# A decode kernel's last weight: W_O loaded in 16, 6, 7, 2, 1 rows, with one piece shared unevenly among the DMA engines

## The chip, the core and the metric

The kernel runs on one core of a Trainium2 chip. The metric is device microseconds (us) of one execution. Before the change three runs gave a median of 195.58 us (195.41 to 195.92).

## The reference

One decoding step of a transformer block in which attention and feed-forward stand side by side: both read the same layer-normed input, and both results are added to `x`. There are 4 sequences, model width 512, 32 query heads over 8 key/value heads of width 128, a window of the last 4096 positions, and a SwiGLU feed-forward of width 1792. All tensors are bf16.

```python
xn = layernorm(x)                                  # 4 x 512
q  = xn @ wq                                       # 4 x 32 heads x 128
k, v = k_cache[:, :, -4096:], v_cache[:, :, -4096:]   # 8 kv heads, each for 4 query heads
o  = softmax(q @ k.T * 128**-0.5) @ v              # per head
a  = o.reshape(4, 4096) @ wo                       # wo: 4096 x 512
f  = (silu(xn @ w_gate) * (xn @ w_up)) @ w_down
return x + a + f
```

The core reads 81 MB from memory, nearly all of it keys and values; `wo` is 4 MB of it.

## The kernel before, in words

The kernel is written engine by engine, with semaphores placed by hand; no scheduler reorders anything. Inside one block each engine has its own program. SP issues every large load in a fixed order: W_Q, then the key and value loads of 16 pairs (kv head, two sequences), each 2 MB, with W_G and W_U among the first and W_down among the last, and at the end W_O. A load is split over the core's 16 DMA engines, and each of them works through its share of all loads in the order of issue. Loads are issued so far ahead that the DMA engines always have work.

TensorE runs, for every pair, transposes of the keys, the scores, the row maximum and P·V, and then the tail: the last pair, the gate and up matmuls, the W_down matmuls, the transposes that put the attention output into the tile `OP`, and the W_O product. The latter is `out_rows`: W_O lies in SBUF as `WO`, 128 partitions by 32 rows `c` of 512 columns (1 KB a row), and for each row `c` two matmuls of 256 columns add `OP[:, c, :]` times that row into the accumulator `ps_acc`. The five pieces in which W_O is loaded are cut at `WO_CUTS`, each with a semaphore of its own `d_wo[n]`, and `out_rows` waits for a piece where its first row comes.

TensorE does the first piece, 16 rows, inside the block. Then come two matmuls whose result nobody reads (`spin`), the end of the block, at which all engines wait for each other, and behind it the other rows. After the last of them VectorE and ScalarE each copy half of `ps_acc` to `y`, and ScalarE's queue stores `y`.

Names used later: `load_wo` issues the pieces of W_O on SP's queue; `d_wo0` to `d_wo4` are their semaphores; `s_op` says that `OP` is written. In the profile the W_O matmuls are `ps_acc<-wo_sb,oP` on line 193, spin matmuls are `ps_s<-kbuf,ident`, and the end of the block is line 197. The load of the W_O pieces stands on line 251.

Of the kernel before, what the change touches and what calls it, by code (L numbers as in the profile page):

```python
# [12 lines left out]
def bass_parallel_sum__sliding_block_cached__swiglu_ffn__decode_kernel(  # L13
# [10 lines left out]
    out: bass.AP,  # L24
):
    B, _, D = A_x.shape
    _, HKV, Sk, Dh = A_k_cache.shape
    HQ = A_wq.shape[1] // Dh
    F = B_w_gate.shape[1]
# [18 lines left out]
    NO = HQ * Dh // 128  # L48
# [11 lines left out]
    WO = sb("wo_sb", [128, NO, D], BF16)  # L60
# [54 lines left out]
    def sem(name):  # L115
        return nc.alloc_semaphore(name=name)
# [3 lines left out]
    d_wu = sem("d_wu")  # L120
    d_wd = sem("d_wd")
    d_out = sem("d_out")
    WO_CUTS = (0, 16, 26, 29, 31, 32)
    d_wo = [sem("d_wo%d" % q) for q in range(len(WO_CUTS) - 1)]
    d_k = [sem("d_k%d" % s) for s in range(2)]
    d_v = [sem("d_v%d" % s) for s in range(2)]
# [30 lines left out]
    s_acc = sem("s_acc")  # L157
# [8 lines left out]
    wo_ap = A_wo.rearrange("(p c) n -> p c n", c=NO)  # L166
# [6 lines left out]
    def load(eng, to, rows, pieces):  # L173


        with nc.discard():
            by_row = eng.dma_start(to, rows).ins
        whole = replace(by_row.ins[0], ap=pieces.ap, bass_ap=pieces)
        return eng.add_instruction(replace(by_row, name=nc.get_next_instruction_name(), ins=[whole],
                                           ant_dge_precooked=False))  # L180

    def fold_rows(w):
        return w.rearrange("(p c) n -> p (c n)", p=32)

    def load_kv(eng, buf, cache, d):
        return load(eng, buf[:, d % 2 * KVN:(d % 2 + 1) * KVN], kv_ap(cache, d, 1), kv_ap(cache, d, FOLD))

    def out_rows(eng, c0, c1):
        for c in range(c0, c1):
            if c in WO_CUTS:  # L190
                eng.wait_ge(d_wo[WO_CUTS.index(c)], 16)
            for n in range(2):
                last = eng.matmul(ps_acc[64 * n:64 * n + B, 0:256], OP[:, c, :], WO[:, c, 256 * n:256 * n + 256],  # L193
                                  start=False, stop=True, skip_group_check=True)
        return last

    with nc.Block() as block:
# [40 lines left out]
        @block.sync  # L238
        def _(eng):
            def load_k(d):  # L240
                if d >= 2:
                    eng.wait_ge(s_tr, 2 * NG * (d - 1))
                load_kv(eng, KB, A_k_cache, d).then_inc(d_k[d % 2], 16)

            def load_v(d):
                eng.wait_ge(s_pv, d + 1)
                load_kv(eng, VB, A_v_cache, d).then_inc(d_v[d % 2], 16)

            def load_wo(n):
                a, b = WO_CUTS[n], WO_CUTS[n + 1]  # L250
                eng.dma_start(WO[:, a:b, :], wo_ap[:, a:b, :]).then_inc(d_wo[n], 16)

            eng.dma_start(WQ[:], wq_ap).then_inc(d_wq, 16)

            eng.wait_ge(s_xc, 1)
            load_k(0)
            load_k(1)
            load(eng, WG[:], wg_ap, fold_rows(B_w_gate)).then_inc(d_wg, 16)
            load(eng, WU[:], wu_ap, fold_rows(B_w_up)).then_inc(d_wu, 16)
            load_v(0)  # L260
            for d in range(2, ND):
                load_k(d)
                load_v(d - 1)
            load(eng, WD[:], wd_ap, fold_rows(B_w_down)).then_inc(d_wd, 16)
            load_v(ND - 1)
            for n in range(len(d_wo)):
                load_wo(n)
# [99 lines left out]
        def _(eng):  # L367
            def mm(o, l, r, start=False, stop=True):
                return eng.matmul(o, l, r, start=start, stop=stop, skip_group_check=True)  # L369
# [65 lines left out]
            def spin(n):  # L435

                for _ in range(n):
                    mm(ps_S[0][:], ident[:], KB[:, 0:512], start=True)
# [6 lines left out]
            with eng.Fori(0, ND // 2) as r:  # L445
                for b in range(2):
                    n = 2 * r + (b + 1)
# [45 lines left out]
            last.then_inc(s_pm, 1)  # L493
            spin(1)
            eng.wait_ge(s_op, 1)
            out_rows(eng, 0, WO_CUTS[1])
            spin(2)

            eng.br_lt(flag, 1, on_true="tensor_tail", on_false="tensor_never")
            with nc.body("tensor_never", valid_engines=[mybir.EngineType.PE]):  # L500
# [2 lines left out]

    out_rows(nc.tensor, WO_CUTS[1], NO).then_inc(s_acc, 1)
    nc.vector.wait_ge(s_acc, 1)
    nc.vector.tensor_copy(y[:, 0:256], ps_acc[0:B, 0:256]).then_inc(s_y, 1)  # L508
    nc.scalar.wait_ge(s_acc, 1)
# [32 lines left out]
```

## Time and profile before

| what | value |
|---|---|
| median of three runs | 195.58 us (195.41 to 195.92) |
| the profiled execution's own time | 195.48 us |
| its span, first to last instruction | 194.2 us |
| TensorE busy | 163.6 us (84%) |
| VectorE busy | 115.2 us (59%) |
| DMA over the span | 81.09 MB, mean 417 GB/s |
| granted TensorE clock, mean | 0.991 |

The span leaves out 1.3 us of the execution's own time, at its two ends. TensorE's busy share is not TensorE at its peak. DMA rates are those of all 16 DMA engines together; a rate over a stretch counts a packet where it starts or lands, so for stretches under a microsecond it is rough. A row of the timeline gives start and length in us, the engine (PE is TensorE's matmul side, PEld its weight load, SPq the queue of DMA issues on SP), line, operation and tiles, a count, and in brackets the idle time before it and who ended it.

### The profile page before, as it was taken

Reading aid. Unit: us, or ns where it says so; the run is one execution under the profiler, and the core shown is the slowest. Engines: PE = TensorE matmul, PEld = TensorE weight load, DVE = VectorE, ACT = ScalarE, POOL = GpSimd, SP = SyncE. Lnnn points to the kernel's source line nnn. Section 1 sums busy time; section 2 is a strip of 40 time slices with the busy share of each in tenths; the row PEclk is TensorE's granted clock in tenths of the full one; section 3 lists DMA queues with packets and bytes.
Section 4 is the critical chain, followed back from the end, with each engine's and each line's share of the span. In section 5 each row is a group of like instructions: output and inputs, shape, how many; then the busy total and the mean of one; then the engine's idle time right before and its main releaser. Section 6 shows DMA issues by size and latency. Waiting matters only on the chain. (4 is left out here: it accounts for less than half of the span.)

```text
span 194.2 us, 7753 instructions
## 1 busy us (share of the span) xinstructions
PE 163.6 (84%) x3462; PEld 141.4 (73%) x3463; DVE 115.2 (59%) x250; ACT 17.0 (9%) x27; POOL 10.5 (5%) x23
## 2 busy tenths in 40 slices
PE   0137999749999989898989898989898989898895
PEld 0112979648989888787878887888788878787663
DVE  1004858517677767676767676767676767675530
ACT  6600010100110101010101010101010101010100
POOL 8930000000000000000000000000000000000000
PEclk9999999988999999999999999999999999999999
DMA  6999997999999999999999999999999999999992
GB/s 217 432 432 432 511 452 326 432 430 439 425 432 432 439 432 432 432 432 439 439 432 432 432 432 432 432 432 439 432 439 432 439 432 432 432 442 429 395 407 94
DMA packets 3589, 81.09 MB, mean 417 GB/s; under 512 B 664, under 2 KB 800, under 8 KB 1056
## 3 DMA queue, kind: packets, MB, share of 16 engines
q1 hardware_dynamic: 3568, 81.01, 97.3%
q8 instruction: 4, 0.07, 0.1%
q10 hardware_dynamic: 16, 0.01, 0.0%
q14 instruction: 1, 0.01, 0.0%
HBM read 81.01 MB, written 0.00 MB: 417 GB/s over the span
## 5 line engine op out<-in xcount | busy, mean ns | idle before, releaser
L311 DVE COPY kT<-ps_kt 128x1024 bf16<-128x1024 bf16 x128 | 79.8, 683 | 28.0 <-PE ps_kt L397 28.0
L397 PE MATMUL ps_kt<-ident,kbuf 128*128 128x128 bf16 x1024 | 65.5, 224 | 11.2 <-DMA kbuf<-in_A_k_cache_dram 10.3
L397 PEld LDWEIGHTS ps_kt<-ident,kbuf 128*128 128x128 bf16 x1024 | 59.9, 101 | 16.5 <-issue 16.5
L369 PE MATMUL ps_o<-p,vbuf 128*128 128x64 bf16 x1120 | 38.4, 193 | 0.0
L369 PEld LDWEIGHTS ps_s<-qz,kT 128*128 128x128 bf16 x1024 | 31.4, 98 | 7.2 <-issue 4.2
L369 PE MATMUL ps_s<-qz,kT 128*128 x1024 | 34.8, 192 | 1.6 <-issue 0.4
L369 PEld LDWEIGHTS ps_o<-p,vbuf 128*128 128x128 bf16 x1120 | 35.2, 98 | 1.1
L282 ACT ACTIVATE p<-ps_s 128x512 bf16<-128x512 f32 x17 | 10.1, 597 | 162.0 <-PE ps_s L369 162.0
L316 DVE TENSOR_REDUCE rm<-ps_s 128x8 bf16<-128x512 f32 x17 | 11.8, 692 | 20.2 <-PE ps_s L369 20.2
L369 PE MATMUL ps_o<-p,ones 128*128 128x128 bf16 (+1 forms) x69 | 7.0, 222 | 2.1 <-DVE qz L302 1.3
L369 PE MATMUL ps_kt<-wq_sb,xnT 128*32 128x512 bf16 x32 | 3.6, 629 | 5.4 <-DMA wq_sb<-in_A_wq_dram 5.4
L369 PEld LDWEIGHTS ps_o<-p,ones 128*128 128x128 bf16 x69 | 4.5, 98 | 3.4 <-issue 2.2
L369 PE MATMUL ps_s<-mkc,mkr 2*128 2x512 bf16 x17 | 6.8, 398 | 0.0
L374 PE MATMUL ps_acc<-i,xn 4*128 4x4 f32 x4 | 0.6, 254 | 7.1 <-ACT xn L279 7.1
L369 PE MATMUL ps_s<-dg,ones 8*128 8x512 bf16 x17 | 6.5, 385 | 0.0
L369 PEld LDWEIGHTS ps_kt<-wq_sb,xnT 128*32 128x32 bf16 x32 | 1.2, 138 | 7.0 <-issue 7.0
L299 DVE STREAM_TRANSPOSE kT<-ps_kt 128x512 f32<-128x512 f32 x2 | 1.4, 717 | 8.1 <-PE ps_kt L369 8.1
L327 DVE TENSOR_REDUCE den<-ps_o 128x8 f32<-128x128 f32 x18 | 5.0, 276 | 1.7 <-PE ps_o L369 1.7
L374 PEld LDWEIGHTS ps_acc<-i,xn 4*128 4x128 f32 x4 | 0.6, 207 | 7.0 <-issue 7.0
L233 POOL MEMSET vbuf<- 128x6144 f32 x1 | 5.2, 5222 | 0.0
L321 DVE TENSOR_REDUCE m<-ps_acc 8x1 f32<-8x128 f32 x17 | 4.6, 270 | 0.3 <-PE ps_acc L369 0.3
L331 DVE TENSOR_TENSOR oT<-ps_o,den 128x8 f32 (+1 forms) x18 | 3.0, 167 | 2.9 <-issue 2.7
(68 smaller groups left out, 49.2 us busy)
## 6 DMA issues: line engine op xcount, KB each, us to landing
kbuf<-in_A_k_cache_dram SPq DMA_DIRECT2D x16, 2048.0 KB, 12.5
vbuf<-in_A_v_cache_dram SPq DMA_DIRECT2D x16, 2048.0 KB, 11.2
wq_sb<-in_A_wq_dram SPq DMA_DIRECT2D x1, 4096.0 KB, 12.1
wo_sb<-in_A_wo_dram SPq DMA_DIRECT2D x1, 2048.0 KB, 14.9
wg_sb<-in_B_w_gate_dram SPq DMA_DIRECT2D x1, 1792.0 KB, 24.3
wu_sb<-in_B_w_up_dram SPq DMA_DIRECT2D x1, 1792.0 KB, 27.7
wd_sb<-in_B_w_down_dram SPq DMA_DIRECT2D x1, 1792.0 KB, 14.9
wo_sb<-in_A_wo_dram SPq DMA_DIRECT2D x1, 1280.0 KB, 17.3
```

What stands on the lines that cost most here:

```text
L233: eng.memset(VB[:, HKN:].bitcast(FP32), 0.0)
L282: eng.activation(P[:, d % 2 * PS:d % 2 * PS + SN], ps_S[d % 2][:], ACT.Exp, scale=SCALE).then_inc(s_p, 1)
L299: eng.transpose(qT[:, 512 * n:512 * n + 512], ps_kt[n][:])
L311: eng.tensor_copy(KT[:, u * HKN + 1024 * g:u * HKN + 1024 * (g + 1)], kt_ps[g].rearrange("p a b -> p (a b)")).then_inc(s_ev, 1)
L316: eng.tensor_reduce(RM[:], ps_S[bank][:].rearrange("p (t c) -> p c t", c=C), AX.X, ALU.max).then_inc(s_rm, 1)
L321: eng.tensor_reduce(m8[:], mt_ps, AX.X, ALU.max)
L327: eng.tensor_reduce(den[:], den_ps.rearrange("p (t c) -> p c t", c=C), AX.X, ALU.add)
L331: eng.tensor_tensor(OT[:, 2 * b:2 * b + 2, ds(r * REP, REP)], O_ps.rearrange("p (j h) -> p j h", j=2), den[:].rearrange("p (j h) -> p j h" ...
L369: return eng.matmul(o, l, r, start=start, stop=stop, skip_group_check=True)
L374: last = eng.transpose(xT_ps[:, c * B:(c + 1) * B], xn[:].rearrange("b (p c) -> b c p", c=NC)[:, c, :], I4[:])
L397: last = eng.transpose(kt_ps[g][:, k, :], KB[:, a:a + 128], ident[:])
```

## The change

W_O is cut at rows 16, 22, 29, 31 in place of 16, 26, 29, 31: the second piece has 6 rows and the third 7, where there were 10 and 3. The 6-row piece is loaded by five DMAs in place of one: every second partition from 0 (64 of them), every fourth from 1 (32), every eighth from 3 (16), and then the 16 partitions 7, 15, ... 127, which are left, in two DMAs whose access patterns are written so that the first 15 are split over five DMA engines, three partitions each, and partition 127 over three engines, a third each. All five add to one semaphore, and the wait is for 80. On TensorE the first 22 rows stand inside the block, where it was 16, and the two spin matmuls behind them are gone.

```diff
-    WO_CUTS = (0, 16, 26, 29, 31, 32)
+    WO_CUTS = (0, 16, 22, 29, 31, 32)
+    WO_SHARES = (1, 5, 1, 1, 1)
...
+    def shared_load(eng, to, rows, k):
+        with nc.discard():
+            by_row = eng.dma_start(to, rows).ins
+        n = to.shape[0]
+        m = to.shape[1] * to.shape[2]
+        s, t = by_row.ins[0].ap[0][0], by_row.outs[0].ap[0][0]
+        if n > 1:
+            of, at = [[n // k * s, k], [s, n // k], [1, m]], [[t, n], [1, 1], [1, m]]
+        else:
+            of, at = [[m // k, k], [1, 1], [1, m // k]], [[t, 1], [m // k, k], [1, m // k]]
+        return eng.add_instruction(replace(by_row, name=nc.get_next_instruction_name(),
+                                           ins=[replace(by_row.ins[0], ap=of, bass_ap=None)],
+                                           outs=[replace(by_row.outs[0], ap=at, bass_ap=None)],
+                                           ant_dge_precooked=False))
...
     def out_rows(eng, c0, c1):
...
-                eng.wait_ge(d_wo[WO_CUTS.index(c)], 16)
+                n = WO_CUTS.index(c)
+                eng.wait_ge(d_wo[n], 16 * WO_SHARES[n])
...
             def load_wo(n):
                 a, b = WO_CUTS[n], WO_CUTS[n + 1]
-                eng.dma_start(WO[:, a:b, :], wo_ap[:, a:b, :]).then_inc(d_wo[n], 16)
+                if WO_SHARES[n] == 1:
+                    eng.dma_start(WO[:, a:b, :], wo_ap[:, a:b, :]).then_inc(d_wo[n], 16)
+                    return
+                for p, step in ((0, 2), (1, 4), (3, 8)):
+                    eng.dma_start(WO[p::step, a:b, :], wo_ap[p::step, a:b, :]).then_inc(d_wo[n], 16)
+                shared_load(eng, WO[7:120:8, a:b, :], wo_ap[7:120:8, a:b, :], 5).then_inc(d_wo[n], 16)
+                shared_load(eng, WO[127:128, a:b, :], wo_ap[127:128, a:b, :], 3).then_inc(d_wo[n], 16)
...
             eng.wait_ge(s_op, 1)
-            out_rows(eng, 0, WO_CUTS[1])
-            spin(2)
+            out_rows(eng, 0, WO_CUTS[2])
...
-    out_rows(nc.tensor, WO_CUTS[1], NO).then_inc(s_acc, 1)
+    out_rows(nc.tensor, WO_CUTS[2], NO).then_inc(s_acc, 1)
```

SP's program at its end, before the change. The shape is partitions by elements, and `wo_sb` is W_O's tile:

```order
34 L177 DMA wd_sb<-in_B_w_down_dram 128x7168
35 L177 DMA vbuf<-in_A_v_cache_dram 128x1x8192
36 L251 DMA wo_sb<-in_A_wo_dram 128x8192
37 L251 DMA wo_sb<-in_A_wo_dram 128x5120
38 L251 DMA wo_sb<-in_A_wo_dram 128x1536
39 L251 DMA wo_sb<-in_A_wo_dram 128x1024
40 L251 DMA wo_sb<-in_A_wo_dram 128x512
```

And with the change, from the same place:

```order
36 L272 DMA wo_sb<-in_A_wo_dram 128x8192
37 L275 DMA wo_sb<-in_A_wo_dram 64x3072
38 L275 DMA wo_sb<-in_A_wo_dram 32x3072
39 L275 DMA wo_sb<-in_A_wo_dram 16x3072
40 L188 DMA wo_sb<-in_A_wo_dram 15x1x3072
41 L188 DMA wo_sb<-in_A_wo_dram 1x3x1024
42 L272 DMA wo_sb<-in_A_wo_dram 128x3584
43 L272 DMA wo_sb<-in_A_wo_dram 128x1024
44 L272 DMA wo_sb<-in_A_wo_dram 128x512
```

The 16-row piece is issued first in both; behind it five DMAs stand for the second piece, and the pieces of 7, 2 and 1 rows follow as nine issues in all.

TensorE's program around the end of the block (the branch on line 197), before the change, where `oP` is `OP`:

```order
85 L369 MATMUL ps_s<-kbuf,ident 128x512
86 L193 MATMUL ps_acc<-wo_sb,oP 4x256 x32
87 L369 MATMUL ps_s<-kbuf,ident 128x512 x2
88 L499 COMPARE_AND_BRANCH
89 L501 COMPARE_AND_BRANCH
90 L197 UNCONDITIONAL_BRANCH
91 L193 MATMUL ps_acc<-wo_sb,oP 4x256 x32
```

And with it:

```order
85 L395 MATMUL ps_s<-kbuf,ident 128x512
86 L213 MATMUL ps_acc<-wo_sb,oP 4x256 x44
87 L524 COMPARE_AND_BRANCH
88 L526 COMPARE_AND_BRANCH
89 L217 UNCONDITIONAL_BRANCH
90 L213 MATMUL ps_acc<-wo_sb,oP 4x256 x20
```

Twelve W_O matmuls have moved from behind the end of the block to ahead of it, in the place of the two spin matmuls.

## The prediction

> **What bounds the kernel now.** The change touches the last 8 us alone, so I read the timeline of both TensorE queues there first. Each row is start, length, engine, line, tiles, count, and in brackets what ended the idle time before it.
>
> ```profile
> 187.81 1.62 PEld L193 LDWEIGHTS ps_acc<-wo_sb,oP 128*4 128x4 bf16 x32 [0.51 <-DVE oP L364]
> 187.81 1.91 PE L193 MATMUL ps_acc<-wo_sb,oP 128*4 128x256 bf16 x32 [0.21 <-DVE oP L364]
> 189.65 0.60 PE L369 MATMUL ps_s<-kbuf,ident 128*128 128x512 bf16 x2
> 190.53 1.66 PEld L193 LDWEIGHTS ps_acc<-wo_sb,oP 128*4 128x4 bf16 x32 [0.76 <-DMA wo_sb<-in_A_wo_dram]
> 190.56 1.91 PE L193 MATMUL ps_acc<-wo_sb,oP 128*4 128x256 bf16 x32 [0.30 <-PEq L197]
> 192.10 0.08 PEld L193 LDWEIGHTS ps_acc<-wo_sb,oP 128*4 128x4 bf16 x2
> 192.51 0.41 DVE L508 CAST y_sb<-ps_acc 4x256 bf16<-4x256 f32 x1 [4.75 <-PE ps_acc L193]
> ```
>
> The first 32 W_O matmuls (16 rows) start at 187.81, when `OP` is there. The spin pair runs until 190.25, then all engines meet, and the other 32 begin with the weight load at 190.53. The last two weight loads come at 192.10, the row that waits for the one-row piece; the copies start at 192.51. Everything after 192.10 is a fixed train: two matmuls, the copies, the store. So the time is set by when 192.10 can be.
>
> Two things could set it. The first is TensorE. One matmul lasts 272 ns in the grouped rows, so 32 of them in 1.91 us start (1.91 - 0.272) / 31 = 0.053 us apart.
>
> ```profile
> L193 PE MATMUL ps_acc<-wo_sb,oP 128*4 128x256 bf16 x64 | 3.8, 272 | 0.5 <-PEq L197 0.3 <-DVE oP L364 0.2
> ```
>
> From 190.53 on, 30 matmuls ahead of the last two take 30 x 0.053 = 1.59, which gives 192.12. The second is the load. The SP queue's rows give the issue, the issue rows the time from there to landing:
>
> ```profile
> 172.17 2.49 SPq L251 DMA_DIRECT2D wo_sb<-in_A_wo_dram  x5
> 172.80 0.43 SPq L251 DMA_DIRECT2D wo_sb<-in_A_wo_dram  x1
> 173.27 0.91 SPq L251 DMA_DIRECT2D wo_sb<-in_A_wo_dram  x2
> 174.22 0.43 SPq L251 DMA_DIRECT2D wo_sb<-in_A_wo_dram  x1
> wo_sb<-in_A_wo_dram SPq DMA_DIRECT2D x1, 2048.0 KB, 14.9
> wo_sb<-in_A_wo_dram SPq DMA_DIRECT2D x1, 1280.0 KB, 17.3
> wo_sb<-in_A_wo_dram SPq DMA_DIRECT2D x1, 384.0 KB, 17.8
> wo_sb<-in_A_wo_dram SPq DMA_DIRECT2D x1, 128.0 KB, 17.8
> ```
>
> The pieces of 16, 10, 3 and 1 rows have landed at 187.07, 190.1, 191.07 and 192.02. So both limits lie at the same place: the one-row piece lands under 0.1 us before it is used, and TensorE arrives there then anyway. A gain needs both to move.
>
> The load does not end on all DMA engines at once. The windows give the rate (last column) with the middle of the loop for comparison:
>
> ```profile
> 100.00:110.00 10.00, 8.93 (x199) 8.00 (x199) 6.92 (x15) 0.60 (x1) 0.00 (x0) 1.00 1.00 433
> 190.00:190.20 0.20, 0.20 (x2) 0.00 (x0) 0.00 (x0) 0.00 (x0) 0.00 (x0) 1.00 0.73 271
> 190.40:190.60 0.20, 0.04 (x2) 0.07 (x4) 0.00 (x0) 0.00 (x0) 0.00 (x0) 1.00 0.35 133
> 191.00:191.20 0.20, 0.20 (x8) 0.17 (x4) 0.00 (x0) 0.00 (x0) 0.00 (x0) 1.00 0.23 87
> 191.40:191.60 0.20, 0.20 (x8) 0.16 (x6) 0.00 (x0) 0.00 (x0) 0.00 (x0) 1.00 0.19 67
> 191.60:191.80 0.20, 0.20 (x8) 0.16 (x6) 0.00 (x0) 0.00 (x0) 0.00 (x0) 1.00 0.06 21
> ```
>
> 433 GB/s over 16 engines is 27.06 GB/s each. 271 GB/s at 190.0 are ten engines, 133 at 190.4 are five, 87 to 67 up to 191.6 are three. Eleven engines are done about 190.4, and four or five work on for another 0.8 to 1.4 us. What made these late is probably the fetching of instructions, which uses the same DMA engines: four packets in the whole run. That is a reading, not shown.
>
> ```profile
> q8 instruction: 4, 0.07, 0.1%
> ```
>
> **The change part by part.** *Unequal shares.* A DMA engine carried 8 partitions of the 6 rows, 6 KB each. With the change every engine carries 7, and the sixteen that are left go to five engines: three each, and for three of those a third of one more. 6 KB at 27.06 GB/s is 0.227 us. Engines outside the five end 0.227 earlier; the five end 2 x 0.227 = 0.45 to 2.33 x 0.227 = 0.53 later. Which engine is late the trace does not say. I take the late ones to lie outside the five, since the other eleven are more than two thirds of sixteen, and cost the opposite below. If the five belong to those done by 190.6, they now end by 191.1, and nobody waits for them.
>
> *Four more DMAs.* SP takes 0.43 us for an issue, so the last one moves from 174.22 to about 176. The data behind them is not moved before the 16-row piece is through, about 187: more than 10 us of cover. Behind the issues SP has nothing but the end of the block at 190. In the DMA engines a piece might cost something of its own: 128 KB came 192.02 - 191.65 = 0.37 behind the 256 KB (issued within the pair at 173.27, that is 173.75, and 17.9 to landing), where 433 GB/s would take 0.30, while 256 KB took 0.58 where it would take 0.61.
>
> ```profile
> wo_sb<-in_A_wo_dram SPq DMA_DIRECT2D x1, 256.0 KB, 17.9
> ```
>
> So a piece costs 0 to 0.07; two more on a late engine 0 to 0.14. I take 0.02, by the 256 KB row. The load's end moves by -0.227 + 0.02 = -0.21.
>
> *The wait inside the block.* TensorE comes to row 16 at 187.81 + 32 x 0.053 = 189.51. A late engine has the 16-row piece at 187.07 and needs 7 x 0.227 = 1.59 more: 188.68. One of the five, late or not, has it by 187.07 + 2.35 = 189.42. No stall, with 0.8 us or 0.1 us to spare.
>
> *Twelve matmuls moved, spin gone.* Inside the block 44 matmuls end at 187.81 + 43 x 0.053 + 0.272 = 190.36, where the spin ended at 190.25. The meeting of the engines is 0.11 later, so the first weight load behind it is ready at 190.64. Then 18 matmuls stand ahead of the last two, not 30: 190.64 + 18 x 0.053 = 191.59, against 192.10. TensorE's own limit moves by -0.51. Spin keeps TensorE busy; the idle stretch that is left, 0.28 us, exists already.
>
> *What is late next.* The 7-row piece ends where the 3-row piece did, 191.07 - 0.21 = 190.86, so TensorE waits 0.2 to 0.3 us behind the end of the block, a wait that was not there. Eighteen matmuls from 190.90 reach 191.85. The one-row piece lands 192.02 - 0.21 = 191.81 and can be used, as now, 0.08 later, at 191.89. That is the limit: 192.10 - 0.21.
>
> The sum against the profiled execution is 195.48 - 0.21 = 195.27. The median of the runs lies 0.10 above that execution, so 195.58 - 0.21 = 195.37.
>
> [...]
>
> **The rivals.** *Loads with a stride over the partitions run slower.* All loads of this trace but 4 KB of `x` and the 4 KB result cover all 128 partitions, and the loop's 433 GB/s is for those. The new loads take every second, fourth or eighth partition, and three or four partitions of a far-off place go to each of the five engines. If two engines then write into the same part of SBUF at one time and halve each other's rate, the 42 KB of an engine take 3.18 in place of 1.59 us. The late engines end 1.59 - 0.21 = 1.38 later than now: in the block TensorE stalls at row 16 until 190.3, and the last piece lands about 193.4. That gives 195.58 + 1.38 = 196.96. The point from which it decides is small: 0.21 / 1.59, so 13% lower rate on this piece, and the gain is gone; 50% longer and it is slower by over 0.3%. For it speaks that 16 engines at 27.06 each show no reserve in the loop that could make up for it; against it that the three strided loads still touch the whole height of SBUF, and that late and early engines are already 1.4 us out of step without disturbing each other. Bounds: 0, and twice the halving where the five also hinder others in the 7-row piece, 195.58 + 2.3 = 197.9.
>
> [...]
>
> *A late engine is among the five.* Then the load ends 0.45 to 0.53 later in place of 0.21 earlier, with three or four small DMAs more: 195.58 + 0.5 = 196.1, still within 0.3%. Five of sixteen are taken, four or five are late; by chance alone one would often be among them. But the one that ends at 191.2, say, could be without harm.
>
> *TensorE's limit counts.* If the load's late end were not so late in an ordinary run, the -0.51 of TensorE would be the gain: 195.58 - 0.51 = 195.07. That is the most there can be. It falls short of 0.3% by a hair (0.59 us). Against it: the late engines stand in the trace, and nothing in the change removes what made them late.
>
> *The change does nothing.* If a piece costs 0.07 in a DMA engine and the strided ones a little more, the time stays at 195.5.
>
> **How the numbers follow.** 0.3% of 195.58 is 0.59 us, about what a measurement of this kernel can tell from no change. Chances: my forecast (-0.21, with the do-nothing case close by) 0.42; a late engine among the five 0.11; strided loads slower 0.40, nearly all of it beyond +0.59; TensorE's limit or something not seen on the fast side 0.07, of which 0.05 beyond 0.3%. Slower is 0.40, faster 0.05, same 0.55. The likeliest case gives 195.37, with a range of its own from 195.1 to 195.7. The whole range begins at TensorE's limit, 195.0 with the scatter of the runs, and goes to 197.2, the halved rate with some of what lies beyond it.
>
> **What would show it.** Right: the weight load behind the end of the block waits for the DMA of W_O and starts near 190.9, the last pair near 191.9, no DMA wait inside the block. Strided loads slow: a DMA wait in the middle of the 44 matmuls, near 189.5, the DMA rate under 430 from 187 to 190, and the last pair at 193 or later. A late engine among the five: no stall in the block, one or two engines moving data until 192.5. Wrong altogether: the stage before 187.8 moves, or TensorE's 0.053 us do.

## The result: slower by 0.28%

The changed kernel takes 196.15 us (median of 17 runs, 196.02 to 196.43) against 195.59 for the kernel before; the ratio is 1.0028, 95% interval 1.0020 to 1.0036. I had forecast 195.37. The loss is 0.56 us.

The profiled execution of the changed kernel took 196.43 us, the longest of its 17, and the one profiled before took 195.48, so the two traces lie 0.95 us apart, some 0.4 us more than the medians. The timeline of TensorE's weight loads from 187 us on (start, length, line, tiles, count, idle time and who ended it; the W_O product is line 213 now):

```profile
187.82 1.65 PEld L213 LDWEIGHTS ps_acc<-wo_sb,oP 128*4 128x4 bf16 x32 [0.52 <-DVE oP L390]
190.21 0.53 PEld L213 LDWEIGHTS ps_acc<-wo_sb,oP 128*4 128x4 bf16 x12 [0.74 <-DMA wo_sb<-in_A_wo_dram]
192.16 1.02 PEld L213 LDWEIGHTS ps_acc<-wo_sb,oP 128*4 128x4 bf16 x20 [1.42 <-DMA wo_sb<-in_A_wo_dram]
193.10 0.08 PEld L213 LDWEIGHTS ps_acc<-wo_sb,oP 128*4 128x4 bf16 x2
```

Up to 187.82 nothing has moved (187.81 before). Then TensorE waits twice for W_O: in the middle of the 44 matmuls, until 190.21, where I had expected the 6-row piece by 188.7 to 189.4, and behind the end of the block until 192.16, where I had expected 190.90. The last pair is at 193.10, 1.00 later than before. So the load is late, not TensorE. Its rate over the stretch in which the 6-row piece moves (last column, GB/s), in the kernel before and in the changed one:

```profile
187.00:189.00 2.00, 1.79 (x27) 1.17 (x27) 0.44 (x1) 0.00 (x0) 0.00 (x0) 1.00 0.97 403
```
```profile
187.00:189.00 2.00, 1.75 (x27) 1.18 (x27) 0.44 (x1) 0.00 (x0) 0.00 (x0) 1.00 1.04 284
```

The DMA engines are as busy as before (the column ahead of the rate, 0.97 and then 1.04 as the share of all sixteen, a rough figure over 2 us), but move 284 GB/s in place of 403. Packets take longer. A packet here is what a DMA engine moves for one partition of a piece (128 packets for each piece of the kernel before). By the packet records of the traces, every packet of the second and third piece takes the same time in the kernel before (385 and 121 ns). In the changed one, 88 of the 128 packets of the 7-row piece and 43 of those of the 6-row piece were stretched, that is took over 15 ns more than the shortest of their piece, all between 186.7 and 190.1 us. The 16-row piece in front of them, which the change leaves as it was, also lands later, 15.6 us behind its issue in place of 14.9:

```profile
wo_sb<-in_A_wo_dram SPq DMA_DIRECT2D x1, 2048.0 KB, 15.6
```

Slower packets are the mark of my first rival, a lower rate on this piece; but the rival blamed the stride, and gave 1.38 us. The experiments ask what exactly is slow.

### The profile page after: what moved, and what is told of

Same layout as the page of the kernel before. It is cut to its first block, busy times and chain, and to the rows that moved or that the text cites. A ratio compares the mean times of both kernels' runs of the same rounds, so it can differ in the third digit from the quotient of the medians.

```text
span 195.2 us, 7753 instructions
## 1 busy us (share of the span) xinstructions
PE 163.3 (84%) x3460; PEld 141.3 (72%) x3461; DVE 115.3 (59%) x250; ACT 17.0 (9%) x27; POOL 10.5 (5%) x23
## 4 chain that ended last, share of the span: by engine, by line
DMA 60%; PE 33%; SPq 2%; issue 2%; DVE 1%; DVEq 0%
DMA kbuf<-in_A_k_cache_dram 46%; PE ps_kt L423 17%; DMA wo_sb<-in_A_wo_dram 8%; PE ps_s L395 8%; DMA wq_sb<-in_A_wq_dram 6%; PE ps_o L395 5%; PE ps_kt L395 2%; SPq L275 1%; SPq L188 1%; PE ps_acc L395 1%; PE ps_acc L213 1%; DVE kT L337 1%; DVE kT L325 0%; SPq L272 0%; SPq L180 0%
## 5 line engine op out<-in xcount | busy, mean ns | idle before, releaser
L213 PE MATMUL ps_acc<-wo_sb,oP 128*4 128x256 bf16 x64 | 4.0, 272 | 1.8 <-DMA wo_sb<-in_A_wo_dram 1.6
L213 PEld LDWEIGHTS ps_acc<-wo_sb,oP 128*4 128x4 bf16 x64 | 2.6, 84 | 3.3 <-DMA wo_sb<-in_A_wo_dram 2.2
## 6 DMA issues: line engine op xcount, KB each, us to landing
wo_sb<-in_A_wo_dram SPq DMA_DIRECT2D x1, 2048.0 KB, 15.6
wd_sb<-in_B_w_down_dram SPq DMA_DIRECT2D x1, 1792.0 KB, 14.9
```

## Experiments

The theories: the *stride* (loads that skip partitions run slower), the *place* (DMA engines that write at one time into one part of SBUF slow each other), the *late engine* (one of the five was among the last), and the *cuts* (the 7-row piece, the moved matmuls). Each ratio is to the kernel before, timed beside it. Where a kernel makes more or fewer loads of the 6-row piece, the count that TensorE waits for (`WO_SHARES`) follows; below, that line is shown for the first kernel only.

**The cuts alone.** The changed kernel, the 6-row piece as one plain load:

```diff
-    WO_SHARES = (1, 5, 1, 1, 1)
+    WO_SHARES = (1, 1, 1, 1, 1)
```

> The changed kernel's cuts (16, 6, 7, 2, 1), its 22 rows inside the block and no spin pair, but the 6-row piece in one load over all 128 partitions like the others. If the uneven sharing or the stride costs the time, this kernel is at 195.6 us or up to 0.1 below (the load's end at 192.0 to 192.1 sets it, TensorE waits for the 7-row piece until 191.1). If the 7-row piece itself or TensorE's new order costs it, it is near 196.1 like the changed kernel, and the 7-row packets are stretched.

Measured: 195.51 us, ratio 1.0004 (0.9986 to 1.0022). Its timeline:

```profile
187.84 2.27 PEld L213 LDWEIGHTS ps_acc<-wo_sb,oP 128*4 128x4 bf16 x44 [0.51 <-DVE oP L390]
191.13 1.08 PEld L213 LDWEIGHTS ps_acc<-wo_sb,oP 128*4 128x4 bf16 x20 [1.02 <-DMA wo_sb<-in_A_wo_dram]
```

The 44 matmuls run without a stop, and TensorE is ready behind the block in good time and waits for the 7-row piece until 191.13. TensorE's gain is eaten by the load, and the time is that of before. No packet of the 6-row or the 7-row piece is stretched. The cuts cost nothing that these runs can tell.

**Strided, but evenly shared.** Four loads on all 16 engines; the five engines' share is gone:

```diff
-                for p, step in ((0, 2), (1, 4), (3, 8)):
+                for p, step in ((0, 2), (1, 4), (3, 8), (7, 8)):
...
-                shared_load(eng, WO[7:120:8, a:b, :], wo_ap[7:120:8, a:b, :], 5).then_inc(d_wo[n], 16)
-                shared_load(eng, WO[127:128, a:b, :], wo_ap[127:128, a:b, :], 3).then_inc(d_wo[n], 16)
```

> The changed kernel with the 6-row piece in four strided loads (every 2nd partition from 0, every 4th from 1, every 8th from 3, every 8th from 7), each over 16 engines, so that every engine again carries 8 partitions. If the stride slows loads, it is as slow as the changed kernel or slower (196.1 or above). If only the five engines' share does, 195.6 to 195.7, with the DMA rate at 430 GB/s from 187 to 189.5. If a late engine among the five is the cause, also 195.6.

Measured: 196.24 us, ratio 1.0052 (1.0025 to 1.0078). As slow with equal shares, so a late engine among the five isn't needed for the loss. The rate from 187 to 189:

```profile
187.00:189.00 2.00, 1.79 (x30) 1.19 (x29) 0.44 (x1) 0.00 (x0) 0.00 (x0) 1.00 1.03 329
```

**A share laid far or near.** The kernel before, with 90 KB more for the five engines behind the 16-row piece, written to a part of W_Q's tile that is out of use. Far is the pattern of the change, near is four neighbouring partitions an engine:

```diff
-            for n in range(len(d_wo)):
+            load_wo(0)
+            shared_load(eng, WQ[:].rearrange("p (c n) -> p c n", n=512)[7:120:8, 16:22, :], wo_ap[7:120:8, 16:22, :], 5).then_inc(d_ex, 16)   # far
+            for n in range(1, len(d_wo)):
...
+            shared_load(eng, WQ[:].rearrange("p (c n) -> p c n", n=256)[0:20, 32:41, :], A_wo.rearrange("(p c) (h n) -> p (c h) n", c=NO, h=2)[0:20, 32:41, :], 5).then_inc(d_ex, 16)   # near
```

> The kernel before with one load more behind the 16-row piece: 15 partitions (7, 15, ... 119), 6 KB each, by the five engines, three partitions each, into a part of W_Q's tile that nobody reads any more. 90 KB more are 0.21 us over 16 engines, 0.68 us on each of the five. If the five hinder the engines that write those partitions otherwise: 0.3 to 1 us over before, with a rate clearly under 430 GB/s while it lasts. If a late engine is among the five and nothing is hindered: 0.5 to 0.7 over before, the same as the next kernel. If neither: within 0.1 of before.

> The same 90 KB on the same five engines, but as four neighbouring partitions each, 0 to 19, 4.5 KB each. [...] If any small load on five engines hinders the rest, it costs as much as the far one.

Measured: far 196.08 us, ratio 1.0027 (1.0014 to 1.0040); near 195.59 us, ratio 0.9997 (0.9985 to 1.0008). The same bytes, on five engines by the same kind of access pattern, cost 0.56 us in one place and nothing in the other. The rate from 185.5 to 187.5, when they move, far and then near:

```profile
185.50:187.50 2.00, 2.00 (x23) 0.96 (x17) 0.69 (x2) 0.00 (x0) 0.00 (x0) 1.00 0.99 308
```
```profile
185.50:187.50 2.00, 2.00 (x25) 1.07 (x19) 0.56 (x2) 0.00 (x0) 0.00 (x0) 1.00 0.99 421
```

The kernel before moves 410 GB/s there. In the trace of the far load 7 of its own 15 packets are stretched, and 60 of the 128 of the 10-row piece behind it; in that of the near load none are, of either.

Two things follow. No engine among the five is so late that 0.68 us more on it moves the end: the late-engine theory is out, for the changed kernel too if its share runs on the same five, which is how it is written; no trace names the engine that moved a packet. And it matters where the five write: both sides are slowed where they write far, while near shares, four neighbours an engine, cost nothing here (195.59 us).

**Which partitions.** The 6-row piece in other parts, all 16 engines, order and cuts as in the changed kernel. In each, the new lines stand in the place of the changed kernel's five loads:

```diff
+                for p in range(4):                                # quarters: every 4th
+                    eng.dma_start(WO[p::4, a:b, :], wo_ap[p::4, a:b, :]).then_inc(d_wo[n], 16)
...
+                for p in range(0, 128, 32):                       # blocks: 32 neighbours
+                    eng.dma_start(WO[p:p + 32, a:b, :], wo_ap[p:p + 32, a:b, :]).then_inc(d_wo[n], 16)
...
+                for p in range(8):                                # eighths: every 8th
+                    eng.dma_start(WO[p::8, a:b, :], wo_ap[p::8, a:b, :]).then_inc(d_wo[n], 16)
```

> The cuts and order of the changed kernel, the 6-row piece in four strided loads of 32 partitions each (every 4th from 0, 1, 2, 3), each over 16 engines. In the trace of the even strided kernel no packet was stretched before the loads of every 8th partition began. If a stride as such slows a load: 196.1 or above. If only loads of 16 partitions do, because two DMA engines then share a part of SBUF: 195.5 to 195.6, with every packet of the piece at 234 ns.

> The same with four loads of 32 neighbouring partitions (0 to 31, 32 to 63, ...), no stride. If strides or the number of DMAs are at fault: 195.5 to 195.7. [...]

> The same with eight loads of 16 partitions (every 8th from 0 to 7). The even strided kernel had two of these and lost 0.7 us. If they are at fault and each costs the same, four times as many lose up to 2.8 us, less where the engines fall out of step: 196.6 to 198.3. If the number of small loads or the five engines' share is at fault instead, 196.0 to 196.3 or no loss.

Measured: quarters 195.41 us, ratio 0.9996 (0.9987 to 1.0005); blocks 200.54, ratio 1.0269 (1.0232 to 1.0306); eighths 199.05, ratio 1.0164 (1.0145 to 1.0183). The rates in the same order:

```profile
187.00:189.00 2.00, 1.79 (x26) 1.16 (x27) 0.44 (x1) 0.00 (x0) 0.00 (x0) 1.00 0.98 411
```
```profile
187.00:189.00 2.00, 0.57 (x5) 0.17 (x3) 0.44 (x1) 0.00 (x0) 0.00 (x0) 1.00 0.95 218
```
```profile
187.00:189.00 2.00, 0.52 (x5) 0.11 (x2) 0.44 (x1) 0.00 (x0) 0.00 (x0) 1.00 0.97 222
```

In the quarters' trace no packet of the two pieces is stretched. The stride theory falls: four loads with a stride cost nothing, four without one are the slowest of all. Eight loads of every 8th partition run at about half the rate, as do blocks of 32 neighbours. The eighths lost more than I expected (3.5 us, not up to 2.8). The blocks lost 5.0 us, more than the 1.8 that half the rate on the 48 KB of an engine would add (48 KB at 27.06 GB/s, an estimate), and so did the one execution of them that has a trace, the fastest of the six (198.88 us, 3.3 over before). Two of its rows, the second its last wait for W_O:

```profile
191.00:192.00 1.00, 1.00 (x14) 0.68 (x10) 0.00 (x0) 0.00 (x0) 0.00 (x0) 0.50 0.81 227
```
```profile
194.57 1.01 PEld L213 LDWEIGHTS ps_acc<-wo_sb,oP 128*4 128x4 bf16 x20 [1.13 <-DMA wo_sb<-in_A_wo_dram]
```

TensorE's granted clock (third column from the end of the first row) was 0.50 from 190 to 193 us, and yet TensorE stood idle for 1.13 us before 194.57 and waited for the 7-row piece. So these 3.3 us are the load's: 103 of the 128 packets of that piece are stretched as well, which the estimate leaves out. Why the other executions took up to 201.70 us no trace shows.

**The rates by themselves.** A kernel of loads alone, one after the other, run once:

```diff
+            eng.dma_start(WO[:], wo_ap[:]).then_inc(d_a, 16)
+            eng.wait_ge(d_a, 16)
+            eng.dma_start(WO[0::2], wo_ap[0::2]).then_inc(d_a, 16)
+            eng.wait_ge(d_a, 32)
+            eng.dma_start(WO[1::4], wo_ap[1::4]).then_inc(d_a, 16)
...
```

> Only loads of W_O, one after the other, each waiting for the one before, and a store of zeros: all 128 partitions (4 MB), every 2nd, every 4th, every 8th partition, the first 64, 32, 16, the two five-engine loads, every 32nd, every 16th, all again; 32 KB per partition. Everything else of the reference is left out. At 27 GB/s per engine: all 9.7 us, every 2nd 4.9, every 4th 2.4, every 8th 1.2, each plus some 2 us. If two engines on one part of SBUF halve each other, every 8th takes 2.4, the first 64 takes 9.7, the first 32 and the first 16 take 4.8 each. If a stride is the cost, the strided ones alone are slow.

SP's waits, in us. A row names the line that waited, that is the issue behind the load: line 62 waits for all 128 partitions, 64 for every 2nd, 66 for every 4th, 68 for every 8th, 70 for the first 64, 72 for the first 32. Line 39, a helper's, waits twice, for the first 16 and then for the five engines' far share; line 78 waits for their near share.

```profile
SPq L62 <- DMA wo_sb<-in_A_wo_dram: 12.0, 1, 12.0
SPq L64 <- DMA wo_sb<-in_A_wo_dram: 6.9, 1, 6.9
SPq L66 <- DMA wo_sb<-in_A_wo_dram: 4.7, 1, 4.7
SPq L68 <- DMA wo_sb<-in_A_wo_dram: 4.4, 1, 4.4
SPq L70 <- DMA wo_sb<-in_A_wo_dram: 12.3, 1, 12.3
SPq L72 <- DMA wo_sb<-in_A_wo_dram: 6.8, 1, 6.8
SPq L39 <- DMA wo_sb<-in_A_wo_dram: 12.1, 2, 6.1
SPq L78 <- DMA wo_sb<-in_A_wo_dram: 6.8, 1, 6.8
```

A load from rest has some 2 us besides its bytes: 12.0 less 9.7 for 4 MB, 6.9 less 4.85 for 2 MB, 4.7 less 2.4 for 1 MB. Every 8th partition, 512 KB, should then take 1.2 + 2.2 = 3.4 and takes 4.4: its bytes go at about half the rate. The first 64 partitions hold as many bytes as every 2nd, and take 12.3 against 6.9: half the rate again, and so do the first 32, 6.8 against 4.7. So every 2nd and every 4th partition run at the full rate, and every 8th, or neighbours, at about half. The packet records say the same: a packet of 32 KB took 1.21 us (median) in the loads of all and of every 2nd partition and 1.30 in that of every 4th, but 2.28 in that of every 8th and 2.56 in those of the first 64 and the first 32. The first 64 ran at 206 GB/s (2.1 MB in 12.3 - 2.1 us), where the loop of the kernel before moves 433. With the 2.2 the slow case of the expectation gives 4.6, 11.9, 7.0 and 7.0 us for every 8th, the first 64, 32 and 16, and 4.4, 12.3, 6.8 and about 6.1 were measured. Three fit; the first 16 run at 0.31 of the 433 (512 KB in 3.9 us, 134 GB/s), where the expected 4.8 us are a quarter. That engines share a part of SBUF in the slow loads no trace shows.

The five engines' shares are not slow by themselves. Far, an engine has three packets, 96 KB or 3.6 us at its full rate, 5.8 with the 2.2, and the load took about 6.1. Near, it has four, and 4.8 + 2.2 = 7.0 stand against 6.8: both times fit five engines, as the access patterns are meant. The median packet took 1.21 us in both. So the far share costs time only beside other loads (0.56 us with the extra far load).

**Parts of the piece.** To size the steps, parts are left out; GpSimd writes zeros to these rows at the start, and the partitions left out keep them.

```diff
+                for p, step in ((0, 4), (1, 4), (2, 4)):          # three quarters; with the two shared loads: the share alone
...
+                for p, step in ((0, 2), (1, 4), (3, 8)):          # with one load of every 8th, no share
```

> Cuts and order of the changed kernel; of the 6-row piece only three loads of every 4th partition (0, 1, 2) are made, and the partitions 3, 7, 11, ... of these rows are zero from the start: a quarter of that piece is left out. Every DMA engine carries 6 partitions, so its load ends 2 x 0.227 = 0.45 us earlier. If the prediction's step holds that the late engines' load sets the end one for one, down to TensorE's own limit at 0.51 less: 195.1. If something else sets the end: 195.5.

> The changed kernel's three strided loads (every 2nd from 0, every 4th from 1, every 8th from 3), without the two loads that the five engines share; the partitions 7, 15, ... of these rows are zero from the start: an eighth of the piece is left out. By the prediction's sum every engine ends 0.21 earlier: 195.3. If the load of every 8th partition costs half of what two of them cost in the even strided kernel (0.7 us): 195.6 to 195.7.

> Three loads of every 4th partition (0, 1, 2) and the five engines' share of 7, 15, ... 127; the partitions 3, 11, ... are zero from the start: an eighth of the piece is left out, and no load of every 8th partition is there. By the sum of engines alone the late ones end 0.45 earlier and the five 0.08 later or less: 195.1. If the share hinders the engines into whose partitions it writes, as the far extra load did (0.5 us): 195.5 to 195.7.

| kernel | us | ratio (95%) | by the sum of engines | loss beyond the sum |
|---|---|---|---|---|
| three quarters | 195.10 | 0.9984 (0.9970 to 0.9998) | -0.45 | 0.0 |
| with every 8th | 195.93 | 1.0022 (1.0010 to 1.0034) | -0.21 | 0.6 |
| share alone | 195.59 | 1.0000 (0.9991 to 1.0009) | -0.45 | 0.5 |
| the whole change | 196.15 | 1.0028 (1.0020 to 1.0036) | -0.21 | 0.8 |

(The first three are timed beside a kernel before of 195.53 us. Each ratio's interval is 0.16 to 0.28 us to either side.) Three quarters give what the sum says, 0.43 us for 0.45: two partitions less per engine end the load that much earlier, and the end follows. The expectation for the share alone puts the five engines 0.08 us later at most; nine partitions in place of eight are 0.23 to 0.30, still under the 0.68 that cost nothing in the near load. The last rows of the three quarters:

```profile
187.80 2.27 PEld L213 LDWEIGHTS ps_acc<-wo_sb,oP 128*4 128x4 bf16 x44 [0.51 <-DVE oP L389]
190.64 1.07 PEld L213 LDWEIGHTS ps_acc<-wo_sb,oP 128*4 128x4 bf16 x20 [0.57 <-DMA wo_sb<-in_A_wo_dram]
190.67 1.26 PE L213 MATMUL ps_acc<-wo_sb,oP 128*4 128x256 bf16 x20 [0.30 <-PEq L217]
```

Here the two limits meet again. The last engine lands the 7-row piece at 190.59, and the matmul row names the end of the block (PEq L217) as its releaser, 0.30 us as in the kernel before (L197): 190.64 is the very time that the prediction gave for TensorE's own limit. So this kernel can't say which of the two holds the end; it shows that both can move that far.

Put the load of every 8th back, and 0.6 us are lost (195.93, where I expected 195.6 to 195.7); put the share in its place, and 0.5 are. Both together lose 0.8, less than their sum, 1.1, though by no more than the intervals allow. Nor is it the slow bytes alone: 6 KB an engine at half the rate are 0.23 us more, and 0.6 are lost. The stretched packets say where the rest goes. With the load of every 8th, 15 of the 112 packets of the 6-row piece are stretched, but 71 of the 128 of the 7-row piece, which is a plain load; with the share, 25 of 111 and 78 of 128; with three quarters, none. Engines that are already at the plain piece are slowed while others still write the split one: in the trace of the changed kernel the 6-row piece is in flight up to 189.39 us, and 70 of the 73 packets of the 7-row piece that start before that are stretched, but 18 of the 55 behind it.

## Why the prediction was wrong, point by point

*What bounds the kernel: right.* Load and TensorE's order meet at the last pair. The cuts alone move TensorE's limit and bring nothing; three quarters of the piece move the load's end too, and bring 0.43 us (0.04 to 0.59).

*Unequal shares, -0.227: this step failed.* It counted bytes per DMA engine, as if an engine's rate were its own. In the runs the rate went with the partitions that are written at one time: in the load of every 8th partition a packet took 2.28 us in place of 1.21, from rest, and the extra share cost time in one place and not in the other (196.08 us far, 195.59 near). The 0.45 to 0.53 for the five rests on their number: no trace names an engine, but the two shares from rest took what three and four packets in a row take, 6.1 and 6.8 us. The load ran at 284 GB/s in place of 403 for 2 us, and the end came 0.8 us later than the sum says. So -0.21 became +0.56.

*Four more DMAs, 0.02: right as far as it is shown.* Quarters make four loads of one, three more and not four, and lose nothing (ratio 0.9996). The cover was less than the prediction says, and enough: the two shared issues took 0.8 us each, so the last issue went out near 177.2 and not 176, and by the packet records the second piece begins to move at 184.9 on the engines that are done first, not at 187.

*The late engines lie outside the five: right for what it was to say.* The near load puts 0.68 us on five engines, meant as the same, and costs nothing. My rival of a late engine among the five, which gave 196.1, has the measured time for the wrong reason: that is luck.

*The wait inside the block: wrong, by the same step.* TensorE stalled until 190.21.

*TensorE's limit: right as a bound.* Behind the end of the block TensorE waited for the load in the traces of all kernels with the new cuts but one. In the three quarters it started at 190.64, at its own limit, as the prediction has it.

*The first rival, "loads with a stride run slower": its halved rate was right in part, its place and its size were not.* Rates about halved there are (packets of 2.28 to 2.56 us for 1.21), and the point from which the rival decides, 13% on this piece, was passed; that engines in one part of SBUF halve each other no run shows. But I hung the loss on the stride, which is harmless by twos and fours, and took the halving for all seven partitions of an engine; only one of the seven, that of every 8th, is of the slow kind, and the share besides. So 1.38 was too much. A halved rate on the one alone is 0.23 us, though, which only eats up the gain of 0.21. What makes 0.56 of it is the share and the plain piece behind; I have no sum that gives that number. The 7-row piece stands in the outer bound of the rival alone, and the bound's 2.3 us is not the twice 1.38 (2.76) that it is said to be.

What stays open: that a share can't help however it is laid, because the partitions of a late engine would have to take the same bytes from another engine, is argued here and not shown. Nor was it shown what made four or five engines late. At 182.4 us of the trace of before sixteen packets are in flight, one of them of instructions (16 KB, 0.95 us), so it takes the time of an engine; that the four such packets account for all the late engines is not shown. And in every run the rows that a load reads from memory go with the partitions that it writes, so no run separates the two; that it is the place in SBUF is my reading.

## What to carry to other kernels

Balance a load by the partitions that its bytes go to, not only by the DMA engine that carries them: where five engines were to help the others, both were slowed (with the extra far load, 7 of its 15 packets and 60 of the 128 behind it were stretched). In these runs loads of every 2nd or every 4th partition cost nothing, and those of every 8th, or of blocks of neighbours, ran at about half the rate. Where two limits meet at one point, as here, size each with an experiment of its own before paying for both.

## What the runs showed of the hardware

A 2 MB load into 64 partitions took 6.9 us with a stride of two and 12.3 us without a stride. That a stride would be the better choice I had not expected. Nor that four DMAs in place of one would be free within 0.13% (ratio 0.9987 to 1.0005), or that one 512 KB load of every 8th partition from rest would take nearly as long (4.4 us) as a 1 MB load of every 4th (4.7 us). The far share, by its access pattern three partitions to each of five engines, ran at full rate alone (1.21 us for a packet of 32 KB), and beside other loads the same pattern cost 0.56 us.
